# Down units of one plain chunk moved to its front, and attention pieces of the first two GLU chunks ordered behind the gate's multiplication

## The chip, the cores and the metric

The kernel runs on one core of a Trainium2 chip. The metric is the device time of the whole program in microseconds (us). The engines are called as in the profile: PE (TensorE matmuls) and PEld (its weight loads), DVE (VectorE), ACT (ScalarE), POOL (GpSimd) and SP (SyncE, which here only issues DMAs). L766 is line 766 of the kernel before; line numbers after the change are a few higher.

## The reference

The input is one sequence of 2048 tokens of width 576, in float32:

```python
h  = x + attn(layernorm(x)) @ wo          # 32 heads of 18, window of 8 keys at distances 0, 2, ..., 14
g  = layernorm(h) @ w_gate                # 576 x 4608
u  = layernorm(h) @ w_up                  # 576 x 4608
h2 = h + (sigmoid(g) * u) @ w_down        # 4608 x 576
```

## The kernel before

The tokens are split by even and odd position and by half into four blocks of 512. Every product is made from split operands: `split` rounds the source on ACT to a high part (L104) and subtracts on DVE for the low part (L105), and a product is three matmuls: high by high, low by high, high by low. So each weight, each activation and each hidden tile costs one ACT and one DVE instruction ahead of its matmuls.

The kernel has three stages. An opening normalises the input and makes q, k and v, with the first attentions beneath it. Then comes the GLU, whose 4608 columns are 36 chunks of 128, in an order written out in `items`. Chunks 0 to 11 are plain chunks ("std") that work for one block only; chunks 12 to 35 are "pair" chunks, which treat two blocks by a scheme of seven products instead of eight, on sums and differences of the blocks' activations (`X["s2"]`, `X["s3"]`, `X["s1"]` and so on); the same order is then run for the other two blocks.

A plain chunk is `single` (L777 on): a gate product of 14 matmuls into PSUM tile b1, its sigmoid on ACT (L790), an up product of 14 matmuls into b2, and `hidden` (L765), which multiplies the two on DVE (L766) and splits the result into h0h and h0l. b1 and b2 have one buffer each: the next chunk's up product may not begin before L766 has read b2.

Every second chunk, the down projection of two chunks is put into `queue` as a generator of four units. One unit (`down_tile`, L860) is 12 matmuls and one add into `stage` (L870). `single` calls `late`, by the name `units`, twice in a chunk: `late(1)` takes one unit, or two where a finished generator still stands ahead of another. Thus even chunks from 4 on take three units and odd ones the remaining unit in the first call, and the second call in an odd chunk only finds the generator finished.

Between its products a chunk calls `side(0)` to `side(5)`, here `twice`, which advances a background generator `bg` by one or two steps through `bg_step`. In the first 12 chunks that is `under_first`: what is left of the attention of block 1, piece by piece, then from chunk 5 on its output projection (`proj_scr`), and then `operands`, the sums that the pair chunks read. One attention has 16 yields: for each half of its tokens a product q times k (L189, 2304 elements a partition), an empty step and a reduction (L193); the softmax (L201 to L207) in two steps; for each half the product with v (L215), an empty step, and two folds (L221, L223). The last add (L226) and the write of the result on POOL's queue (L228) come with the step that begins the next attention and issues its q, k and v loads on SP (L176 to L178). When chunk 0 begins, one piece (L223) and the last add of one attention are left, and two whole attentions after it. Chunk 0 takes eight such steps: L223; then L226 with L189 of the first half, and an empty one; L193; L189 of the second half; after L766 in the program an empty one and L193; and the softmax's first step.

The order on each engine is not the order of the program. A planner lists the instructions ahead of time by priority and by when it expects them to be ready; `high_priority(HC)` or `(HI)` lifts what stands under it, and the engine then runs its list strictly in that order. `issue_after(ins)` orders all instructions written under it behind `ins` on the engine of `ins`, here DVE, without adding a wait on another engine. `skip` names the sides at which `bg_step` does nothing while attention is under way.

Buffers: the raw weights of a chunk come through `load_gu` (L702, tile wg, two buffers, two chunks ahead); the split weights w1 have two buffers, w2 and w4 one each; the split down weights d have four, so those of chunks 10 and 11 take the places of chunks 6 and 7, whose units chunk 8 and chunk 9 finish.

Of the kernel before, what the change touches and what calls it, by code (L numbers as in the profile page):

```python
# [18 lines left out]
ALU = mybir.AluOpType  # L19
# [31 lines left out]
END = object()  # L51
# [3 lines left out]
NSTD = 12  # L55
# [5 lines left out]
def kernel(ctx, tc, x, wqkv, wo, wmlp, out):  # L61
    nc = tc.nc
    dve, act, pool, pe, sp = nc.vector, nc.scalar, nc.gpsimd, nc.tensor, nc.sync

    def sb_pool(name, side="left"):
        return tc.tile_pool(name=name, bufs=1, side=side, reuse_waits="tile")
# [233 lines left out]
    def x_half(raw, rest):  # L300
        t = tl_tile() if rest is None else th_tile()
        split(t[:, 0:2], t[:, 2:4], raw)
        if rest is not None:
            split_rest(t[:, 4], rest)
        return t
# [394 lines left out]
    def load_gu(f, eng=sp, n=WC):  # L700
        ws = gw.tile([P, WC], F32, bufs=2, name="wg")
        behind[0] = eng.dma_start(ws[:, :n], wmlp[f][:, :n])  # L702
        return ws

    def paced(dst, src):
        with tc.issue_after(getattr(behind[0], "ins", behind[0])):
            behind[0] = sp.dma_start(dst, src)
# [33 lines left out]
    def prod(ps, xx, w, n, first):  # L741
        wt, k0 = w[n]
        k = 0
        for c in range(2):
            for a, m in ((0, 0), (0, 2), (1, 0)):
                pe.matmul(ps, wt[:, a, k0 + c], xx[:, m + c], start=first and k == 0,  # L746
                          stop=k == 5, skip_group_check=True)
                k += 1

    def rest(ps, xx, w, n):  # L750
        wt, k0 = w[n]
        for a in range(2):
            pe.matmul(ps, wt[:, a, k0], xx[:, 4], start=False, stop=a == 1,  # L753
                      skip_group_check=True)
# [3 lines left out]
    def halves(name, src):  # L758
        n = 3 if name == "h0" else gc_bufs
        hh = gc.tile([P, TB], F32R, bufs=n, name=name + "h")  # L760
        hl = gc.tile([P, TB], F32R, bufs=n, name=name + "l")
        split(hh, hl, src)
        return hh, hl

    def hidden(sg, ps, name):  # L765
        dve.tensor_tensor(sg, sg, ps, ALU.mult)  # L766
        return halves(name, sg)

    def s_tile():
        return gh.tile([P, TB], F32, tag="s", bufs=4, name="s")  # L770

    def b_tile(i):
        return gp.tile([P, TB], F32, name=f"b{i % 3 + 1}")
# [7 lines left out]
    def single(X, w, t, units, side):  # L781
        xa, xb = (X["a00"], X["a01"]) if t == 0 else (X["a10"], X["a11"])
        pg, pu = b_tile(0), b_tile(1)
        prod(pg, xa, w, "b00", True)
        side(0)
        prod(pg, xb, w, "b10", False)
        rest(pg, xb, w, "g4")
        sg = s_tile()
        with tc.high_priority(HC):
            act.activation(sg, pg, AF.Sigmoid)  # L790
        side(1)
        units(1)
        side(2)
        prod(pu, xa, w, "b01", True)
        side(3)
        prod(pu, xb, w, "b11", False)
        rest(pu, xb, w, "u4")
        with tc.high_priority(HC):
            hid = hidden(sg, pu, f"h{t}")
        side(4)  # L800
        units(1)
        side(5)
        return {t: hid}

    added = [None]
    gated = [None]
# [218 lines left out]
    def under_first():  # L1025
        wos = [None, None]
        for _ in ag:
            if c >= 3 and wos[1] is None:
                wos[1] = wos_early()
            yield ATT  # L1030
        at_stk.close()
        a1 = xt.tile([P, 5, TB], F32, tag="th", bufs=3, name="ar")
        with sb_pool("pj", "right") as pj:
            while c < 5:
                yield
            yield from proj_scr(pj, 1, a1, wos)
        with sb_pool("pp", "right") as pp:
            yield from operands(pp, 0, X, ("s2", "s3", "s1", "a11", "s4"), None, a1)
# [3 lines left out]
    c = 0  # L1042
# [35 lines left out]
    def bg_step(i):  # L1078
        nonlocal raw, phase
        if phase is ATT and i in skip:  # L1080
            return
        r = next(bg, END)
        phase = ATT if r is ATT else None
        if isinstance(r, dict):
            raw = r

    def finish_bg():
        while True:
            r = next(bg, END)
            if r is END:  # L1090
                return
            if isinstance(r, dict):
                set_raw(r)
# [7 lines left out]
    def units(n):  # L1101
        for _ in range(n):
            while queue:
                if next(queue[0], END) is END:
                    queue.pop(0)
                else:
                    break
# [6 lines left out]
    bg = under_first()  # L1114
# [70 lines left out]
    def last_sums(f):  # L1185
        def last(h0, h1):
            if f % 2 == 0:
                M["a00"] = halves("h0", hid_raw("00", *h0))
                hid_raw("10", *h1)
            else:  # L1190
                M["a01"] = halves("h0", hid_raw("01", *h0))
                hid_raw("11", *h1)
        return last
# [17 lines left out]
    def lag(n):  # L1211
        for _ in range(n):
            yield
# [22 lines left out]
    def twice(i):  # L1236
        bg_step(i)
        if i in (1, 4) or phase is not ATT and i in (2, 5):
            bg_step(i)

    for c, (kind, p, f) in enumerate(items):
        w, d = wc
        for b, late_c in ((0, NF + NSTD - 3), (1, NF + NSTD + 5)):
            if c == late_c:
                e, hf = BLOCKS[b]
                paced(ov[e, hf], hacc[b])
        skip = () if kind == "std" else (3,)
        by_seven = c >= NF + NSTD
        if c == NSTD:
            finish_bg()  # L1250
            last_x = splits[-1]
            bg = under_rest(getattr(last_x, "ins", last_x))
        if c == NF + NSTD:
            finish_bg()
            with tc.high_priority(HI):
                for n in ("s1", "a11"):
                    Xn[n] = x_half(*raw[n])
            X = Xn
            pp_stk.close()
            dw = ctx.enter_context(sb_pool("dw", "right"))  # L1260
        if c == 0:
            wc = wc_next
        elif c + 1 < len(items):
            wc = weights(items[c + 1][0], wg, c + 1 < NF + NSTD)
        if c + 2 < len(items):
            wg = load_gu(items[c + 2][2], n=WC if c + 2 < NF + NSTD else GU)
        hid = {}
        blocks = [p] if kind == "std" else [2 * p, 2 * p + 1]

        def last(h0, h1):  # L1270
            hid[0] = hidden(*h0, "h0")
            hid[1] = hidden(*h1, "h1")

        if kind == "std":
            hid = single(X, w, p, late, twice)
        elif not by_seven:
            side = last_pair if c == NF - 1 else bg_step

            def between(i):
                if i in (4, 6):  # L1280
                    units(2)
                side(i)

            pair(X, w, between, last)
        else:
            def between(i):
                nonlocal st, gc, gc_bufs, dk
                units(1)
                if c == NF + NSTD and i == 5:
                    assert not queue  # L1290
                    st_stk.close()
                    gc_stk.close()
                    gc = gc_stk.enter_context(sb_pool("gc2"))
                    st = st_stk.enter_context(sb_pool("st2"))
                    dk = dk_stk.enter_context(sb_pool("dk", "right"))
                    for n in ("s4h", "s4l", "s1h"):
                        dk.tile([P, TB], F32R, name=n)
                    gc_bufs = 2
                down_side(f, i)

            pair(X, w, between, last if f >= NF - NPL else last_sums(f))
            if f < NF - NPL:
                if f % 2:
                    if f == 1:
                        queue.append(lag(LAG))
                    queue.append(seven())
                continue
            d = M[f]
        seg.append((hid, d))
        if len(seg) == 2:  # L1310
            if by_seven and f == NF - NPL + 1:
                queue.append(load_tails())
            for b in blocks:
                queue.append(down_std(seg, b, f // 2) if kind == "std" else
                             down_tail(seg, b, f == NF - 1) if by_seven else down_units(seg, b))
            seg = []
# [44 lines left out]
```

## Time and profile before

| | us |
|---|---|
| three runs | 1581.74, 1587.62, 1590.11 (median 1587.62) |
| the profiled execution | 1584.15 |
| its span, from first to last instruction | 1582.2 |
| PE busy | 1551.0 (98%) |
| DVE busy | 1256.3 (79%) |
| ACT busy | 881.1 (56%) |
| mean granted clock of PE | 0.996 |

The plain chunks for the first block run from about 221 to 358 us. In a timeline row the first number is the start, the second the duration (from the first start to the last end, where several instructions are merged), then come engine, line, operation and tiles; in square brackets stands how long the engine was idle before it, and what ended that. A row by stages gives the window, its length, then the busy time of PE, PEld, DVE, ACT and POOL with instruction counts, the granted clock, the share of DMA time and GB/s.

### The profile page before, as it was taken

What the parts mean: (1) busy time and instruction counts of PE and PEld (TensorE: products, weight loads), DVE (VectorE), ACT (ScalarE), POOL (GpSimd) and SP (SyncE); (2) the same over time, 40 slices, a digit from 0 to 9 for tenths busy, and PEclk for the clock granted to TensorE, in tenths of its full rate; (3) what the DMA queues carried; (4) which work ended last, traced back from release to release, by engine and by line L of the source; (5) the groups of instructions that cost most, each with busy time, mean ns of one, the idle gap of its engine ahead of it and who ended that gap; (6) DMA issues with size and microseconds to landing.
All of it is one profiled execution on the core that took longest, in us unless ns stands there. A gap on an engine that the chain in (4) does not pass through costs nothing.

```text
span 1582.2 us, 22358 instructions
## 1 busy us (share of the span) xinstructions
PE 1551.0 (98%) x8520; PEld 1378.4 (87%) x8520; DVE 1256.3 (79%) x1883; ACT 881.1 (56%) x1584; POOL 199.0 (13%) x249
## 2 busy tenths in 40 slices
PE   8999989999999999999999999999999999999998
PEld 7899878887888888888888888888888888888888
DVE  6998999869999999999526588876777776677755
ACT  6631234425655655555543445767777776677761
POOL 2300000020000010000101010112112211112210
PEclk9999999999999999999999999999999999999999
DMA  8646544645457667664584524899999989989983
GB/s 276 216 168 220 186 185 166 222 165 171 118 147 195 166 170 186 165 165 109 138 239 151 181 81 126 185 180 177 171 180 186 175 169 185 176 169 181 185 175 121
DMA packets 77148, 273.96 MB, mean 173 GB/s; under 512 B 8336, under 2 KB 14224, under 8 KB 76144
## 3 DMA queue, kind: packets, MB, share of 16 engines
q0 software_dynamic: 28192, 107.29, 37.6%
q1 hardware_dynamic: 41216, 145.11, 27.2%
q10 hardware_dynamic: 7632, 20.12, 3.3%
q8 instruction: 66, 1.08, 0.3%
q14 instruction: 42, 0.34, 0.1%
HBM read 143.98 MB, written 130.87 MB: 174 GB/s over the span
## 4 chain that ended last, share of the span: by engine, by line
PE 85%; DVE 9%; DMA 4%; ACT 1%; issue 1%; POOL 0%; ACTq 0%; SPq 0%; POOLq 0%; DVEq 0%
PE b L746 43%; PE dp L860 15%; PE dp L922 11%; PE b L753 8%; PE acc L157 4%; DMA wg<-in_wmlp_dram 2%; DVE lg L193 2%; DVE pr L189 2%; PE b L157 1%; PE bgp L157 1%; DVE pr L215 1%; DMA kw<-k 1%; DMA h<-z 1%; DVE pr L221 1%; DMA k<-ev 1%
## 5 line engine op out<-in xcount | busy, mean ns | idle before, releaser
L746 PE MATMUL b<-tl,w 128*128 128x512 f32 x1704 | 433.5, 394 | 3.6 <-ACT s L816 2.0
L746 PEld LDWEIGHTS b<-tl,w 128*128 128x128 f32 x1704 | 309.4, 189 | 60.8 <-ACT s L816 3.1
L746 PE MATMUL b<-th,w 128*128 128x512 f32 x1344 | 346.9, 393 | 3.1 <-DVE s L766 3.1
L746 PEld LDWEIGHTS b<-th,w 128*128 128x128 f32 x1344 | 245.3, 188 | 48.3 <-DVE s L766 3.6
L928 ACT ACTIVATE ev<-dp 128x576 f32<-128x576 f32 x224 | 144.7, 646 | 63.0 <-PE dp L922 58.6
L753 PE MATMUL b<-th,w 128*128 128x512 f32 x568 | 176.3, 391 | 0.0
L104 ACT ACTIVATE w<-wg 128x384 fp32r<-128x384 f32 (+1 forms) x186 | 110.7, 601 | 112.7 <-PE b L753 54.4
L931 POOL DMA_DIRECT2D h<-ev x128 | 110.1, 860 | 458.5 <-ACT ev L928 444.7
L157 PE MATMUL acc<-qw,th 128*128 128x432 f32 x512 | 154.4, 362 | 3.0 <-DVE th L109 2.2
L105 DVE TENSOR_TENSOR w<-wg,w 128x384 fp32r<-128x384 f32 (+1 forms) x186 | 121.0, 656 | 38.4 <-ACT w L104 38.0
L105 DVE TENSOR_TENSOR w<-tw,w 128x512 fp32r<-128x512 f32 x120 | 82.6, 688 | 82.1 <-ACT w L104 81.4
L753 PEld LDWEIGHTS b<-th,w 128*128 128x128 f32 x568 | 107.0, 188 | 23.3
L860 PE MATMUL dp<-d,h1h 128*128 128x288 f32 x640 | 118.8, 295 | 0.0
L860 PE MATMUL dp<-d,h0h 128*128 128x288 f32 x608 | 112.1, 295 | 0.7 <-DVE tail L870 0.7
L868 ACT ACTIVATE stage<-dp 128x576 f32<-128x576 f32 x104 | 67.2, 647 | 71.4 <-PE dp L860 70.7
L157 PEld LDWEIGHTS acc<-qw,th 128*128 128x128 f32 x512 | 96.9, 189 | 8.7 <-DVE th L109 3.4
L860 PEld LDWEIGHTS dp<-d,h1h 128*128 128x128 f32 x640 | 98.7, 188 | 3.0
L104 ACT ACTIVATE w<-tw 128x512 fp32r<-128x512 f32 x120 | 75.4, 628 | 42.6 <-PE b L746 39.9
L860 PEld LDWEIGHTS dp<-d,h0h 128*128 128x128 f32 x608 | 93.9, 189 | 4.0 <-DVE tail L870 1.0
L157 PE MATMUL acc<-qw,tl 128*128 128x432 f32 x256 | 92.8, 363 | 0.1
L189 DVE TENSOR_TENSOR pr<-kw,q 128x2304 f32<-128x2304 f32 x32 | 81.8, 2555 | 9.7 <-DMA kw<-k 9.5
L876 POOL DMA_DIRECT2D h<-stage x26 | 31.0, 1193 | 438.5 <-ACT stage L868 337.3
(310 smaller groups left out, 2953.4 us busy)
## 6 DMA issues: line engine op xcount, KB each, us to landing
h<-ev POOLq DMA_DIRECT2D x96, 576.0 KB, 6.9
wg<-in_wmlp_dram SPq DMA_DIRECT2D x47, 928.0 KB, 5.8
h<-stage POOLq DMA_DIRECT2D x26, 1152.0 KB, 10.7
wg<-in_wmlp_dram SPq DMA_DIRECT2D x36, 640.0 KB, 4.2
kw<-k SPq DMA_DIRECT2D x16, 792.0 KB, 4.8
vw<-v SPq DMA_DIRECT2D x16, 792.0 KB, 4.7
wd<-in_wmlp_dram SPq DMA_DIRECT2D x18, 576.0 KB, 7.4
h<-ev POOLq DMA_DIRECT2D x32, 288.0 KB, 6.8
```

Source lines behind the costliest of these rows:

```text
L104: act.activation(hi, src, AF.Copy)
L105: splits.append(dve.tensor_tensor(lo, src, f32(hi), ALU.subtract))
L157: pe.matmul(ps[:, :n], a[:, c, js], m[:, c], start=k == 0, stop=False)
L189: dve.tensor_tensor(pr, both(kw, u), q[:, us].unsqueeze(2).broadcast_to([P, 2, W, CG]), ALU.mult)
L193: dve.tensor_reduce(lg[:, us].rearrange("p j w h -> p (j w h)"), pr.rearrange("p j w (h d) -> p (j w h) d", d=DH), AX.X, ALU.add)
L746: pe.matmul(ps, wt[:, a, k0 + c], xx[:, m + c], start=first and k == 0, stop=k == 5, skip_group_check=True)
L753: pe.matmul(ps, wt[:, a, k0], xx[:, 4], start=False, stop=a == 1, skip_group_check=True)
L860: pe.matmul(ps[:, i, :DH2], a[:, js], d[:, m, i * DH2:(i + 1) * DH2], start=k == 0, stop=k == n)
L868: act.activation(hv, ps, AF.Copy)
L922: pe.matmul(ps[:, i, :DH2], a[x][:, js], m[y], start=k in (0, 1, 3) and q == 0, stop=q == 2, skip_group_check=True)
L928: act.activation(hs[:, k % 2], ps[:, :, :DH2], AF.Copy)
L931: pool.dma_start(hsev[:, u, k0:k + 1], hs[:, :k + 1 - k0], accum_op=ALU.add, max_dma_last_dim=8 * D)
```

## The change

Two edits. In chunk 9 (`c == NSTD - 3`, the third-last plain chunk of the first pass) the call for down units that stood after `side(1)` stays, the one after `side(4)` is dropped, and one is added between the two halves of the gate product. So the one unit that is left there is issued at the front. In chunks 0 and 1 every attention step that is taken once a gate multiplication exists is written under `issue_after` of the latest one; `hidden` now records that multiplication in `gated`. In chunk 0, attention also takes no step at sides 2 and 3.

```diff
     def hidden(sg, ps, name):
-        dve.tensor_tensor(sg, sg, ps, ALU.mult)
+        m = dve.tensor_tensor(sg, sg, ps, ALU.mult)
+        gated[0] = getattr(m, "ins", m)
         return halves(name, sg)
...
         prod(pg, xa, w, "b00", True)
         side(0)
+        if c == NSTD - 3:
+            units(1)
         prod(pg, xb, w, "b10", False)
...
         side(4)
-        units(1)
+        if c != NSTD - 3:
+            units(1)
         side(5)
...
-        r = next(bg, END)
+        with ExitStack() as way:
+            if c < 2 and gated[0] is not None:
+                way.enter_context(tc.issue_after(gated[0]))
+            r = next(bg, END)
         phase = ATT if r is ATT else None
...
-        skip = () if kind == "std" else (3,)
+        skip = ((2, 3) if c == 0 else ()) if kind == "std" else (3,)
```

## The prediction

> **What bounds the kernel.** I read the page first, then who waits for whom on the matmul engine, then the timeline where those waits lie.
>
> ```profile
> span 1582.2 us, 22358 instructions
> PE 1551.0 (98%) x8520; PEld 1378.4 (87%) x8520; DVE 1256.3 (79%) x1883; ACT 881.1 (56%) x1584; POOL 199.0 (13%) x249
> ```
> PE is busy 1551.0 of 1582.2 us, and the change neither adds nor removes a matmul. So it can only win back PE's idle time and what follows from it, or add to it.
>
> ```profile
> PE b L746 <- DVE s L766: 8.4, 3, 4.0
> ```
> The largest wait of a GLU product is for L766, the gate's multiplication: three waits, 8.4 us. Now the first of the three, in chunks 0 and 1:
>
> ```profile
> 225.44 2.55 DVE L193 TENSOR_REDUCE lg<-pr 128x128 f32<-128x2304 f32 x1
> ...
> 227.02 0.62 PE L753 MATMUL b<-th,wf 128*128 128x512 f32 x2
> ...
> 228.38 2.55 DVE L189 TENSOR_TENSOR pr<-kw,q 128x2304 f32<-128x2304 f32 x1
> ...
> 230.19 0.61 PE L753 MATMUL b<-th,wf 128*128 128x512 f32 x2
> ...
> 231.52 2.55 DVE L193 TENSOR_REDUCE lg<-pr 128x128 f32<-128x2304 f32 x1
> 234.09 0.69 DVE L766 TENSOR_TENSOR s<-s,b 128x512 f32<-128x512 f32 x1
> ...
> 234.84 2.93 PE L746 MATMUL b<-tl,wf 128*128 128x512 f32 x6 [4.03 <-DVE s L766]
> ```
> Chunk 0's up product ends at 227.64 (227.02 + 0.62), so its multiplication could start there. DVE takes its instructions in the order written, and three attention pieces stand ahead of it, so it starts at 234.09. Chunk 1's gate product ends at 230.80; its up product needs the bank that the multiplication reads, and waits 4.03 us.
>
> ```profile
> 234.84 5.49 PE b L746 x12
> ...
> 250.38 2.75 PE b L746 x12
> ```
> From the chain that ended last: the twelve products after that wait take 5.49 us, twelve like them at 250.38 take 2.75. The wait thus costs 2.74 us more in slow matmuls, 6.77 in all.
>
> The other two waits lie where the plain chunks give way to the pair chunks:
>
> ```profile
> 330.22 0.52 PE L860 MATMUL dp<-d,h0h 128*128 128x288 f32 x2
> ...
> 331.30 1.47 ACT L104 ACTIVATE d<-wg 128x576 fp32r<-128x576 f32 x2 [0.20 <-PE dp L860]
> ...
> 335.30 0.63 PE L753 MATMUL b<-th,w 128*128 128x512 f32 x2
> ...
> 337.23 0.56 DVE L105 TENSOR_TENSOR w<-wg,w 128x384 fp32r<-128x384 f32 x1
> ...
> 337.81 0.33 SPq L702 DMA_DIRECT2D wg<-in_wmlp_dram  x1
> ...
> 344.99 0.61 PE L753 MATMUL b<-th,w 128*128 128x512 f32 x2
> ...
> 348.54 0.69 DVE L727 TENSOR_TENSOR tw<-wg 128x512 f32<-128x512 f32 x1 [6.77 <-DMA wg<-in_wmlp_dram]
> ...
> 352.36 0.68 DVE L766 TENSOR_TENSOR s<-s,b 128x512 f32<-128x512 f32 x1
> ...
> 353.18 1.61 PE L746 MATMUL b<-tl,w 128*128 128x512 f32 x6 [1.21 <-DVE s L766]
> ...
> 359.71 1.22 DVE L105 TENSOR_TENSOR tl<-ar,tl 128x1024 fp32r<-128x1024 f32 x1
> ...
> 361.98 0.68 DVE L766 TENSOR_TENSOR s<-s,b 128x512 f32<-128x512 f32 x1
> ...
> 362.72 2.60 PE L746 MATMUL b<-th,w 128*128 128x512 f32 x6 [3.14 <-DVE s L766]
> ...
> 365.97 4.55 PE L746 MATMUL b<-tl,w 128*128 128x512 f32 x18
> ```
> Chunk 9's remaining down unit starts at 330.22, behind the projection. The splits of two down weights wait for it on ACT (331.30). The up product of chunk 9 ends at 335.93; only then can chunk 10's single-buffered w4 be split (337.23 to 337.79), and that split is the last reader of the buffer into which the load at 337.81 goes. DVE stands still 6.77 us for this load, with chunk 10's multiplication behind it: due at 345.60 (344.99 + 0.61), it starts at 352.36. PE then waits 1.21 and 3.14 us.
>
> ```profile
> 362.00:380.00 18.00, 17.28 (x86) 15.04 (x87) 16.17 (x27) 8.96 (x15) 0.00 (x0) 0.91 0.53 205
> ```
> The granted clock over these 18 us is 0.91: another 18 x 0.09 = 1.62 us. The boundary costs 1.21 + 3.14 + 1.62 = 5.97 us. Both places together hold 12.7 us, the most that the change can bring by these rows.
>
> The Trainium skill, "TensorE: Matmul & The Clock Gate", Part 1, says that an idle window of about 3.4 us halves the clock and that some 3.4 us of work restores it. The trace agrees in kind: 4.03 us of waiting cost 2.74 more, 3.14 cost 1.62, and 1.21 left 1.61 us for six products. By that rule a new single wait above 3.4 us would cost an estimated 1.7 us on top, and the sum below would end 1.7 us higher.
>
> **The ties in chunks 0 and 1.** Nothing is removed; DVE's order changes. Counted along the generator's yields, chunk 0 now gets L193 of the first half, L189 of the second and (the third row above, at 231.52) L193 of the second half, two of them ahead of its multiplication in the program. Afterwards steps 2 and 3 are skipped, so only L189 of the first half stays ahead; it was done before 225.44. The rest carries the tie. The multiplication starts near 227.7, chunk 1's up product at 230.80, and 6.77 us return. A wait is added: behind the multiplication stand the tied pieces, DVE has only two short weight splits left from 225.4 to 227.7 and idles for about 1 us of it, and everything of attention waits for that. The next multiplication is at worst one 2.55 us piece late and is needed only after chunk 2's gate product, so I price that at nothing; without that cover it would be 2.55.
>
> The price is the attention's end.
>
> ```profile
> 234.84:298.46 63.62, 63.62 (x328) 55.53 (x329) 61.71 (x77) 32.22 (x53) 0.71 (x1) 0.96 0.42 148
> ```
> ```profile
> L105 DVE TENSOR_TENSOR w<-wg,w 128x640 fp32r<-128x640 f32 (+2 forms) x21 | 12.1, 598 | 0.6 <-ACT w L104 0.5
> ...
> L870 DVE TENSOR_TENSOR stage<-stage,dp 128x576 f32<-128x576 f32 x8 | 6.0, 748 | 0.0
> ...
> L105 DVE TENSOR_TENSOR h0l<-s,h0h 128x512 fp32r<-128x512 f32 x7 | 4.8, 686 | 0.0
> L766 DVE TENSOR_TENSOR s<-s,b 128x512 f32<-128x512 f32 x7 | 4.8, 683 | 0.3 <-PE b L753 0.2
> L105 DVE TENSOR_TENSOR d<-wg,d 128x576 fp32r<-128x576 f32 x6 | 4.5, 751 | 0.0
> ```
> ```profile
> 297.71 0.75 DVE L226 TENSOR_TENSOR kw<-kw 128x576 f32<-128x576 f32 x1
> ...
> 302.37 1.75 SPq L707 DMA_DIRECT2D oj<-o  x4
> ```
> DVE is busy 61.71 of the 63.62 us to the attention's end (297.71 + 0.75 = 298.46). The chunks' own work there is 12.1 + 6.0 + 4.8 + 4.8 + 4.5 = 32.2, about half. With PE 6.77 us ahead, 0.5 x 6.77 = 3.4 us of it comes earlier, and attention, which gets the other half, ends 3.4 / 0.5 = 6.8 us later by the clock. The idle microsecond ahead of the tie adds to it: (3.4 + 1.0) / 0.5 = 8.8. Bounds: 3, if DVE's present gaps (1.9 us) and short pieces take up most; (3.4 + 5.1) / 0.5 = 17, if two tied pieces of 2.55 us leave DVE idle for their full length. I take 8.8, since DVE has next to no gap. The projection's loads follow that end (302.37).
>
> SP is in order too:
>
> ```profile
> 251.24 0.32 SPq L178 DMA_DIRECT2D vw<-v  x1
> 252.30 0.33 SPq L702 DMA_DIRECT2D wg<-in_wmlp_dram  x1
> ```
> The v window waits for an attention piece on DVE, and chunk 5's weights are queued behind it. A few us later here is hidden by PE's two chunks of distance, between 0 and 2 us; I take 0.
>
> **The unit of chunk 9.** The projection's products lie ahead of it on PE, and the loads of that time meet the zero writes:
>
> ```profile
> 315.25 1.59 PE b L157 x12
> ...
> 328.18 1.58 PE bgp L157 x12
> ...
> 340.16 9.63 DMA h<-z
> ...
> 370.98 3.18 PE dp L860 x24
> ```
> Of the two calls that move, one finds only the finished generator; one unit of 12 matmuls goes from 330.22 to between the two halves of chunk 9's gate product. PE's total stays. Its add on DVE and the down weights' splits (1.47 on ACT and their halves on DVE) leave the crowded stretch from 330 to 337; the unit's tile of PSUM is free by then, as its last but one is added. No DMA is issued by it. Alone, with PE's order as it is, chunk 9's up product would still end at 335.93 and the load would come at most 1.5 us sooner: the low bound, about 1. With the projection 8.8 us later, however, PE finds the up product of chunk 9 before the projection's products (315.25 to 329.8), w4 is free up to 15 us earlier, and the load lands before the crowd: the whole 5.97. I take this one, because the late attention forces that order.
>
> **What is late next.** The pair chunk's second sum. Its split ends at 360.93 (359.71 + 1.22), its product is the second third of the row at 365.97, about 367.4. Without the 6.77 us of standing still it is ready at 354.2, plus 8.8 = 363.0; PE, 12.7 us earlier, wants it at 354.7. That is 8.3 us. PE can fill 3.2 of it with the two down units that now follow at 370.98 and depend on no sum; 5.1 remain. They fall in pieces on the first two sums, each near the waits of 1.21 and 3.14, so the clock adds between 0 and 1.6; I take 0.
>
> **Sum.** 6.77 + 5.97 - 5.1 = 7.6 us won. The profiled execution took 1584.15, with its span of 1582.2 and 1.95 around it: 1576.5. The median of the runs, 1587.62, lies 3.5 above it, inside their spread of 8.4; I stay with the profiled one and let the upper end hold the rest.
>
> **Rivals.**
> *All of it is kept.* DVE's gaps and an earlier start of the sums absorb the delay: 1584.15 - 12.7 = 1571.4. For it: around 345 DVE waits for a load rather than for work. Against it: it has nearly no gap before 298. 0.20.
> *It cancels.* The load stays behind the zero writes, so the second sum is ready at 360.9 + 8.8 = 369.7 against 367.4 - 6.8 = 360.6: 9.1 - 3.2 = 5.9 lost for 6.8 won, 1583.3. For it: a planner decides the order on PE and DVE, and here it put DVE behind a load. 0.15.
> *Slower.* The tied pieces leave DVE idle and attention ends 17 us late; the second sum comes at 377.9 against 360.6, 17.3 - 3.2 = 14.1 lost in one long wait, with 2.7 of slow matmuls behind it as at 234.84, for 6.8 won: 1594.2. It decides from an attention end about 15 us late (313.5 on). For it: DVE is full. Against it: weights and down adds can fill in. 0.13.
> That the tie does nothing can't be: L766 would have to stay behind pieces that are now ordered after it.
>
> **Chances.** The forecast has 0.52. About 0.5% (8 us) is what a measurement of this kernel can tell from no change. The forecast's own spread, 4 to 11 us won, lies half on either side of that: faster is 0.20 + 0.26 = 0.46, same 0.26 + 0.15 = 0.41, slower 0.13. The range goes from 1570 (all kept, less 1.4 of spread between runs) to 1590 (cancelled, at the level of the slower runs), and leaves out most of the slower case and a little below.
>
> **What would show it.** Right: the wait of 4.03 us and the slow products behind it gone; L766 of chunk 0 ahead of its L193; attention's last L226 some 3 to 10 us later by the clock; the load of chunk 12 issued well before the zero writes; a wait of PE at the pair chunk's first sums. Wrong: L226 near 298 with no wait after it (more won), a long wait of DVE for the weights still there (cancelled), or PE waiting for weights in chunks 2 to 6.

## The result, and the profile after

The changed kernel takes 1580.92 us (median of 22 runs, 1576.39 to 1588.99); the kernel before, in 22 runs beside them, 1584.88 (1581.46 to 1590.11). The ratio is 0.9978, 95% interval 0.9969 to 0.9987: about 3.5 us less (0.0022 x 1584.88), 2 to 5 by the interval. 7.6 us were forecast.

The profiled execution of the changed kernel took 1584.01 us, above that median, and has the same span as the one of before. Its page:

```profile
span 1582.2 us, 22347 instructions
PE 1551.0 (98%) x8520; PEld 1377.3 (87%) x8520; DVE 1255.2 (79%) x1883; ACT 879.2 (56%) x1584; POOL 199.9 (13%) x249
```

Equal spans hide what moved. The start of the k-th matmul, set against the k-th of before, shows it: from the 1000th to the 1300th (198.7 to 262.5 us of before) PE wins 6.2 us; from there to the 2000th (391.3) it gives 2.3 back on balance; to the 2150th (419.6) another 2.9; after that the two programs are the same, and differ only as executions do. First the front, in the timeline:

```profile
227.15 0.69 DVE L766 TENSOR_TENSOR s<-s,b 128x512 f32<-128x512 f32 x1 [1.25 <-PE b L753]
227.75 2.55 DVE L193 TENSOR_REDUCE lg<-pr 128x128 f32<-128x2304 f32 x1
...
229.60 0.62 PE L753 MATMUL b<-th,wf 128*128 128x512 f32 x2
...
230.05 1.52 PE L746 MATMUL b<-tl,wf 128*128 128x512 f32 x6
```

L766 of chunk 0 now stands ahead of its L193, and chunk 1's up product follows its gate product with no wait. DVE's idle time for the tie is the 1.25 us in brackets.

Next, who waits for whom on PE. The row for L766 (8.4 us in three waits) is gone altogether. Of the next two rows the first is new, and the second has grown (L820 is L816 of the kernel before, where the row had 2.0 us in two waits, the longest 1.8):

```profile
PE b L146 <- DMA oj<-o: 4.2, 1, 4.2
PE b L746 <- ACT s L820: 3.2, 3, 2.4
```

The first lies where the attention hands over to its projection:

```profile
307.78 0.75 DVE L226 TENSOR_TENSOR kw<-kw 128x576 f32<-128x576 f32 x1
...
309.27 0.33 SPq L702 DMA_DIRECT2D wg<-in_wmlp_dram  x1
309.46 0.82 POOL L230 DMA_DIRECT2D o<-kw  x1
...
311.01 0.61 PE L753 MATMUL b<-th,w 128*128 128x512 f32 x2
...
314.63 0.42 PE L864 MATMUL dp<-d,h0h 128*128 128x288 f32 x2
314.89 0.29 PE L864 MATMUL dp<-d,h0l 128*128 128x288 f32 x1
...
316.44 1.75 SPq L707 DMA_DIRECT2D oj<-o  x4
...
319.42 1.11 PE L146 MATMUL b<-ident,oj 128*128 128x128 f32 x4 [4.23 <-DMA oj<-o]
```

Attention ends at 308.53. POOL's queue then writes its last result, and the projection's first load (316.44) waits for that write to land, 6.85 us in the chain of waits. In the same moment, at 309.27, SP has sent the 928 KB of a chunk's weights (chunk 11's, counting on from chunk 5's load). Chunk 9's up product ends at 311.62 (the row at 311.01, found by counting products from chunk 0), so the projection does stand behind it in PE's list now. Its first transposes (L146) stand in chunk 10, three matmuls into a down unit. PE is there at 315.2, and 4.23 us pass with the rest of that unit and chunk work queued behind. The DMA issues of 292 to 326 us, first before, then after (KB and us to landing last):

```profile
o<-kw POOLq DMA_DIRECT2D x1, 128.0 KB, 2.9
```
```profile
o<-kw POOLq DMA_DIRECT2D x1, 128.0 KB, 6.9
```

By stages (window, length, busy time of PE, PEld, DVE, ACT, POOL, then the clock):

```profile
314.31:317.73 3.42, 0.88 (x6) 0.56 (x4) 1.49 (x2) 1.79 (x3) 0.00 (x0) 1.00 0.18 16
317.73:321.14 3.41, 1.72 (x8) 1.72 (x9) 0.00 (x0) 0.57 (x1) 0.00 (x0) 0.50 0.92 327
321.14:324.55 3.41, 3.41 (x16) 3.35 (x16) 1.50 (x3) 0.98 (x3) 0.00 (x0) 0.50 1.03 402
```

For 6.8 us after the wait's middle the clock is granted at half, and 1.72 + 3.41 us of PE's work in it take twice as long: 2.6 us more. The place costs 4.23 + 2.6 = 6.8 us.

The longest of the waits for L820, 2.37 us, lies behind a load of weights:

```profile
380.85 0.76 DVE L105 TENSOR_TENSOR d<-wg,d 128x576 fp32r<-128x576 f32 x1
...
381.67 0.33 SPq L702 DMA_DIRECT2D wg<-in_wmlp_dram  x1
...
390.53 0.74 ACT L104 ACTIVATE w<-wg 128x640 fp32r<-128x640 f32 x1 [4.38 <-DMA wg<-in_wmlp_dram]
...
392.68 0.57 ACT L820 ACTIVATE s<-b 128x512 f32<-128x512 f32 x1
...
393.31 3.01 PE L746 MATMUL b<-tl,w 128*128 128x512 f32 x12 [2.37 <-ACT s L820]
```

The load (chunk 15's by the same count; the expectations call it chunk 14's) lands after 8.8 us. ACT has the split of these weights ahead of L820 in its list, which copies a finished product out of PSUM, and stands 4.38 us; PE's next product goes into the bank that this copy reads, so PE needs the copy, not the weights, and stands 2.37. In the kernel before the load was sent at 379.75 and landed in 4.5 us. What differs is a transfer sent just ahead of it, in the DMA issues of after, 378 to 395:

```profile
h<-stage POOLq DMA_DIRECT2D x1, 1152.0 KB, 10.5
wg<-in_wmlp_dram SPq DMA_DIRECT2D x1, 928.0 KB, 8.8
```

### The profile page after: what moved, and what is told of

It is laid out like the page before. It is cut to its first block, busy times and chain, and to the rows that moved or that the text cites. A ratio compares the mean times of both kernels' runs of the same rounds, so it can differ in the third digit from the quotient of the medians.

```text
span 1582.2 us, 22347 instructions
## 1 busy us (share of the span) xinstructions
PE 1551.0 (98%) x8520; PEld 1377.3 (87%) x8520; DVE 1255.2 (79%) x1883; ACT 879.2 (56%) x1584; POOL 199.9 (13%) x249
## 4 chain that ended last, share of the span: by engine, by line
PE 58%; issue 16%; DVE 11%; DMA 8%; POOL 4%; ACT 2%; SPq 0%; ACTq 0%; POOLq 0%; DVEq 0%
PE b L746 27%; PE dp L864 13%; PE dp L926 6%; PE b L753 5%; PE acc L157 4%; POOL h L935 3%; DMA wg<-in_wmlp_dram 3%; DVE pr L189 2%; DVE pr L215 1%; DVE lg L193 1%; DVE w L105 1%; DVE pr L221 1%; PE b L157 1%; PE bgp L157 1%; DMA x<-tok 1%
## 5 line engine op out<-in xcount | busy, mean ns | idle before, releaser
L105 DVE TENSOR_TENSOR w<-wg,w 128x640 fp32r<-128x640 f32 (+1 forms) x186 | 120.8, 656 | 41.3 <-ACT w L104 41.1
```

What stands on the lines that cost most here:

```text
L105: splits.append(dve.tensor_tensor(lo, src, f32(hi), ALU.subtract))
```

## The experiments

The theory (A): the ties win the front, and by making attention late also the boundary, because PE's list then has chunk 9's up product ahead of the projection; the moved unit adds nothing; the price is the projection's first load, and what follows from it. The rivals differ in which part acts and where time is lost.

| kernel | ratio, 95% interval | PE against before, 1000th-1300th / -2000th / -2150th matmul, us |
|---|---|---|
| the change | 0.9978 (0.9969 to 0.9987) | -6.2 / +2.3 / +2.9 |
| ties and skip only | 0.9988 (0.9975 to 1.0001) | -6.1 / -1.7 / +4.4 |
| the same again | 0.9980 (0.9967 to 0.9992) | -5.8 / -0.6 / +4.4 |
| unit only | 1.0005 (0.9991 to 1.0019) | -0.1 / +2.4 / 0.0 |
| change, no skip | 1.0028 (1.0012 to 1.0044) | -3.6 / +5.8 / 0.0 |
| change, write by SP | 0.9990 (0.9977 to 1.0003) | -6.3 / -2.0 / +6.7 |
| change, projection from chunk 6 | 0.9954 (0.9938 to 0.9970) | -6.2 / -3.8 / +2.1 |
| the same again | 0.9952 (0.9935 to 0.9969) | -6.2 / -3.9 / +2.3 |
| ties, skip, projection from chunk 6 | 0.9974 (0.9959 to 0.9989) | -6.3 / -2.8 / +2.2 |
| the same again | 0.9962 (0.9946 to 0.9978) | -6.3 / -1.5 / +2.1 |
| before, projection from chunk 6 | 0.9993 (0.9980 to 1.0005) | -0.3 / -2.6 / +4.0 |
| change, sums on POOL | 0.9972 (0.9959 to 0.9985) | -6.4 / +4.2 / +0.6 |
| that, projection from chunk 6 | 0.9979 (0.9965 to 0.9993) | -6.3 / -0.6 / +6.0 |

The last column comes from one profile of each kernel, k-th matmul against k-th, good to about 1 us where the order differs; between profiles of unchanged code the 1000th matmul alone moves by up to 2.9 us, so only differences after it are used.

**The ties and the skip alone.**

```diff
-        if c == NSTD - 3:
-            units(1)
...
-        if c != NSTD - 3:
-            units(1)
+        units(1)
```

> Only the ties and the skipped steps of chunks 0 and 1; chunk 9's unit stays where it was. Theory A (late attention alone reorders PE, and the whole loss is one wait for the projection's first load): the 4.03 us wait at the front is gone as after the full change, attention ends about 10 us late, the first transpose still waits 4 to 5 us for its load, the two waits at the boundary for the gate's multiplication are gone although the unit was not moved; time within 1.5 us of the full change, 0.997 to 0.999 of before. Rival B (the moved unit is what clears the boundary): the waits of 1.2 and 3.1 us at the boundary are still there, some 5 us slower than the full change, 1.000 to 1.001 of before.

Measured: 0.9988; repeated, with this expectation:

> The change without the moved unit once more (12 runs gave 0.9988, 0.9975 to 1.0001, against 0.9978 with it). Theory A, the unit's place is worth nothing once the ties are there either: 0.997 to 0.999, and together with the first twelve runs within 0.001 of 0.9978. Rival C, the unit is worth 1.5 to 3 us beside the ties: 0.9985 to 1.000.

Measured: 0.9980. PE's waits of the first (the repeat has 2.5 and 2.8 in their places):

```profile
PE b L746 <- ACT s L817: 2.8, 2, 2.6
PE b L146 <- DMA oj<-o: 2.7, 1, 2.7
```

No wait for L766 is left, at the front or the boundary, though the unit stands where it stood. So both gains come from the ties and the skip. The wait at the projection is 2.7 us and not the 4 to 5 expected; the write of 128 KB ahead of it lands in 5.4 us here, against 6.9 in the change. Against the whole change the two results leave 1.6 and 0.3 us for the unit (0.0010 and 0.0002 of 1584), inside the intervals.

**The unit alone.** The diff of the change without its parts in `hidden`, `bg_step` and `skip`.

> Only the move of chunk 9's unit; attention as before. Theory A: the 4.03 us wait at the front is there, the projection's products still lie ahead of chunk 9's up product, chunk 12's load is issued at most 1.5 us sooner than 337.8, DVE still stands for it; 0 to 2 us won, 0.9985 to 1.000 of before. Rival B: the boundary's waits of 1.2 and 3.1 us vanish, about 6 us won, 0.996.

Measured: 1.0005, no difference, and the waits for L766 are the ones of before to the digit:

```profile
PE b L746 <- DVE s L766: 8.4, 3, 4.0
```

**The ties without the skip.**

```diff
-        skip = ((2, 3) if c == 0 else ()) if kind == "std" else (3,)
+        skip = () if kind == "std" else (3,)
```

> The change without its skipped steps: chunk 0 takes its attention steps at sides 2 and 3 again, the ties and the moved unit stay. Theory A: chunk 0's two pieces of 2.55 us that stand ahead of its multiplication in the program are not tied, so L766 of chunk 0 starts near 234 again and PE waits about 4 us there; what is gained is gained from chunk 1 on. Attention then ends nearer to 298 than to 308 (300 to 304), the projection's load is no longer late (no wait above 2 us for oj<-o), and the boundary decides: with PE's order as before the change 6 us are kept at most, ratio 0.997 to 1.001. Rival D, the ties alone clear the front and the skip is only there to spread the steps: the 4.03 wait is gone, ratio at 0.9978 or lower.

Measured: 1.0028, slower than before, outside both expectations. Attention ends at 299.67, hardly late, but:

```profile
231.89 1.66 PE L746 MATMUL b<-tl,wf 128*128 128x512 f32 x6 [1.49 <-DVE s L766]
...
308.25 1.11 PE L146 MATMUL b<-ident,oj 128*128 128x128 f32 x4 [3.04 <-DMA oj<-o]
...
354.82 1.60 PE L746 MATMUL b<-tl,w 128*128 128x512 f32 x6 [1.37 <-DVE s L766]
...
364.35 1.85 PE L746 MATMUL b<-th,w 128*128 128x512 f32 x6 [3.14 <-DVE s L766]
```

The front keeps 1.49 of its 4.03 us (about 4 expected), and both boundary waits are back (1.37 and 3.14; before 1.21 and 3.14), with chunk 9's up product behind the projection's products again (it ends at 337.3; 335.9 before, 311.6 in the change). The projection's load is waited for too, which was not expected: PE is 4 us early and the attention is not. This is the sharpest result: without lateness the boundary is not won, and being early at the projection costs what the front won. The skip is what makes the ties pay.

**The last write by SP's queue.**

```diff
-            pool.dma_start(oscr[b][:, :, g * CG:(g + 1) * CG], o)
+            eng = sp if (b, g) == (1, 3) else pool
+            eng.dma_start(oscr[b][:, :, g * CG:(g + 1) * CG], o)
...
-                pool.dma_start(oscr[b][:, :, D:DX], o[:, :, CG - DR:CG])
+                eng.dma_start(oscr[b][:, :, D:DX], o[:, :, CG - DR:CG])
```

> The full change, with the last attention's result written through SP's queue instead of POOL's. Theory A: the write lands some 3 us after its issue instead of 6.9, the projection's load follows 3 to 4 us sooner, the 4.2 us wait of the first transpose falls below 1.5 us and no slow matmuls follow it; 3 to 7 us won against the full change, 0.994 to 0.996 of before. Rival C (the pair chunk's sums are the price whatever the load does): the wait moves to the pair chunk's products, no change against the full change, 0.998.

Measured: 0.999, so the expected gain did not come, though the first part of its mechanism did:

```profile
o<-kw SPq DMA_DIRECT2D x1, 128.0 KB, 2.9
```
```profile
PE b L146 <- DMA oj<-o: 2.0, 1, 2.0
```

The write lands in 2.9 us as in the kernel before, and the wait falls from 4.23 to 2.0 (below 1.5 expected). The projection's load is now sent at 310.79, with a load of weights 2.3 us ahead of it, and takes 5.7 us to land in place of 2.9. PE reaches the 2000th matmul 4.3 us earlier than in the change, and gives 6.7 back by the 2150th: a wait of 2.79 us at 387.2 and halved clock from 390.0 to 396.9. The second place takes what the first releases.

**The projection one chunk later.**

```diff
-            while c < 5:
+            while c < 6:
                 yield
```

> The full change, with the projection's steps taken from chunk 6 on instead of chunk 5, so that PE's list has its first transposes 18 products and most of a unit (about 5 us) later, while the load itself comes when it did. Theory A: PE works through the 4.2 us in which it stood, no slow matmuls; 4 to 7 us won against the full change, 0.994 to 0.996 of before. Rival C: the projection's later steps come later too, and PE stands for the pair chunk's sums instead; 0 or a loss against the full change, 0.998 to 1.000.

Measured: 0.9954. PE's longest wait for oj<-o is 0.2 us, and the stage from 305 to 330 reads, first in the change, then here:

```profile
305.00:330.00 25.00, 20.77 (x104) 17.68 (x103) 14.49 (x26) 9.19 (x19) 1.45 (x2) 0.86 0.67 246
```
```profile
305.00:330.00 25.00, 24.84 (x141) 21.52 (x140) 21.30 (x37) 12.25 (x25) 1.45 (x2) 1.00 0.71 256
```

PE does 141 matmuls in place of 104. The attention ends at 312.84 by this profile's clock, which is 3.5 us behind that of the change at the 1000th matmul already, so it is about as late as there; but the transposes stand later in PE's list (321.21), and PE does not wait for them. With the sole hindrance at that place gone, the change is worth 7.3 us (0.0046 x 1584; 5 to 10 by the interval), close to the 7.6 forecast (whether by its working is asked below). It beats the kernel before; its interval and that of the change (0.9969 to 0.9987) barely touch. Its repeat:

> The kernel with the putting off to chunk 6 once more, in five rounds beside the two others, since its six runs and the twelve without the moved unit (0.9974, 0.9959 to 0.9989) overlap. Theory A, the unit's place is worth nothing: 0.9955 to 0.998, the same as without it. Rival C, the unit is worth 2 to 3 us here: 0.9945 to 0.996.

Measured: 0.9952.

**The same line on the kernel before.**

> The kernel before, with the projection's first step put off from chunk 5 to chunk 6 (the one line of the last experiment, without the change). Theory A: the kernel before has no wait for the projection's load (its write lands in 2.9 us, no row of oj<-o among PE's waits), its stall is the three waits for L766, 8.4 us, of which the front's 4.03 stays whatever happens at chunk 5. The later projection can at most free PE's order at the boundary, as the late attention did: between nothing and the 5.97 us of the boundary, so a ratio of 0.996 to 1.002, with the first of the three L766 waits kept in any case. If it gains nothing, the 1576.93 us of the last experiment needs the ties. Rival B: the putting off is the whole gain and the change adds nothing to it: 1576.9 here as well, ratio 0.9954.

Measured: 0.9993, no difference shown; rival B falls. PE's waits:

```profile
PE b L746 <- DVE s L766: 5.2, 3, 4.0
PE b L746 <- ACT s L816: 2.8, 3, 2.2
```

The front's 4.0 stays. Of the boundary's 4.35 us (1.21 + 3.14) at most 1.2 is left: a late projection clears it without any tie, which supports the reading that the order on PE, not the unit, is what matters there. The 2.6 us so won return at chunk 15's weights (the second row, with +4.0 in the table).

**The ties and the later projection, without the unit.** The diffs of the first and the fifth experiment together.

> The change without the moved unit, and the projection's first step put off to chunk 6. Theory A: the unit's place is worth nothing, so this is as fast as with it: a ratio of 0.994 to 0.997, no wait for oj<-o and none above 2 us for L766. Rival C: the unit, moved to the front, is what PE does instead of waiting once the projection is later; without it 1.5 to 4 us of waiting come back in chunks 9 to 12, ratio 0.997 to 1.000.

Measured: 0.9974, with a repeat:

> The ties and the putting off to chunk 6, without the moved unit, once more (0.9974, 0.9959 to 0.9989 in twelve runs, against 0.9954 and 0.9952 with the unit). Theory A: 0.994 to 0.9965, the difference was chance. Rival C: 0.9968 to 0.999 again, and the unit's place is worth some 3 us in this kernel.

Measured: 0.9962. Here the unit is not idle after all. Its first profile (the second has 2.6):

```profile
PE b L146 <- DMA oj<-o: 2.7, 1, 2.7
```

In both, PE again stands at the transposes; in both profiles with the unit at the front (0.9954, 0.9952) the wait is at most 0.2 us, since the transposes stand behind a whole unit. So with the later projection the unit covers a wait of 2.6 us. Rival C holds in the traces; the times agree (some 2.4 us between the means) but the intervals overlap, so its size stays open.

**Three of the pair chunks' sums on POOL.**

```diff
-        dve.tensor_tensor(s3, a00, a10, ALU.subtract)
+        eng.tensor_tensor(s3, a00, a10, ALU.subtract)
...
-        dve.tensor_tensor(s4, a01, s2, ALU.subtract)
+        eng.tensor_tensor(s4, a01, s2, ALU.subtract)
...
-        dve.tensor_tensor(rd, a0[:, 4], a1[:, 4], ALU.subtract)
+        eng.tensor_tensor(rd, a0[:, 4], a1[:, 4], ALU.subtract)
```

> The change with three of the five sums ahead of the pair chunks (L285, L287 and L289, 1.22, 1.22 and 0.69 us of DVE) done by POOL. Theory A: what the change gives back at chunk 14 (2.9 us between the 2000th and the 2150th matmul, of which 2.37 are a wait for a split of weights whose load SP issues at 381.67, released by DVE) comes from DVE, 17.70 of 18 us busy there. With 3.1 us taken from DVE that load is issued 2 to 3 us sooner and the wait falls below 1 us; the 4.23 us wait for oj<-o stays. Ratio 0.995 to 0.997. Rival E: POOL is slower and the sums get later, so PE waits in chunk 12 for a split of a sum, 2 us or more: ratio 0.998 to 1.001. Rival F: the load at chunk 14 is not DVE's doing; nothing moves, ratio 0.9978.

Measured: 0.9972, not to be told from the change. The test of DVE's part did not work, for two reasons in one profile:

```profile
354.94 2.81 POOL L285 TENSOR_TENSOR ar<-ar,ar 128x1024 f32<-128x1024 f32 x1 [1.16 <-DVE rs L283]
357.70 3.36 POOL L287 TENSOR_TENSOR rs<-ar,rs 128x1024 f32<-128x1024 f32 x1
```
```profile
382.08 0.33 SPq L702 DMA_DIRECT2D wg<-in_wmlp_dram  x1
```

A sum that takes DVE 1.22 us takes POOL 2.8 to 3.4, and PE now waits three times in chunk 12: 1.8 and 1.2 us for copies out of PSUM (L820, L830) and 1.2 for the split of a sum, so rival E holds in part (2 us or more for a sum's split). And the load that should have come 2 to 3 us sooner came at 382.08, against 381.67. With the later projection the same edit does not help either:

> The same three sums on POOL, with the projection's first step put off to chunk 6. Theory A: both places where the change gives time back are gone; against the putting off alone (0.9954) 1 to 2 us more, ratio 0.993 to 0.995. Rival E: sums on POOL too late, a wait in chunk 12, ratio 0.996 to 1.000.

Measured: 0.9979 (0.9965 to 0.9993), against 0.9952 (0.9935 to 0.9969) without it: likely worse, though the intervals just overlap. PE waits 1.2 and 1.4 us for splits of sums in chunk 12, and 2.9 us at 387.9 for the copy L820, which ACT has behind a load of weights; the stage around it has a clock of 0.83:

```profile
380.00:400.00 20.00, 17.11 (x68) 13.82 (x67) 14.50 (x19) 6.48 (x12) 0.00 (x0) 0.83 0.33 95
```

Whether a shorter DVE list at 350 to 380 would win chunk 15's wait is not shown; what both runs show is that PE waits for these sums when POOL makes them.

## Why the prediction was right or wrong

**The front: right.** 6.77 us were expected, 6.2 measured, and 5.8 to 6.4 in every kernel with ties and skip. L766 of chunk 0 starts at 227.15 (227.7 expected), chunk 1's up product at 230.05 (230.80, with the whole stretch 0.6 earlier in this profile).

**The boundary: right in its cause and its size.** DVE's standing still for the load, PE's waits of 1.21 and 3.14 and the half clock behind them are gone; chunk 12's load is sent at 320.85 instead of 337.81. That the late attention does this, and the unit alone does nothing, was the choice made there, and the first three experiments bear it out. This profile's account closes with the 6.0 us in full: 8.3 us were lost between the 1300th and the 2000th matmul (6.8 at the projection, and 0.86, 0.44 and 0.20 in three short waits), and 8.3 - 6.0 is the 2.3 of the table. The low bound of about 1 us for the unit alone was no measurable gain.

**The attention's end: right.** 8.8 us later by the clock was taken, 10.1 measured (308.53 against 298.46), within 3 to 17. The working holds in the main: from 222 us (221.35 in the change, whose profile is 0.65 early) to that end DVE is busy 82.49 us in place of 74.49, 8.0 more with the same attention in it, and idle 2.7 more; of the 8.8 worked out, 1.0 was idle time and the other 7.8 chunk work. What the skipped steps add to this was no term of its own, and they matter: without them the attention ends at 299.67, only 1.2 later.

**What is late next: this step failed, in two terms.** It looked for the first work that needs the late attention, named the pair chunk's second sum, and took 5.1 us off for it. It put the wait for the projection's load at nothing. It had noted that "the projection's loads follow that end", and rightly took the projection's products to stand behind chunk 9's in PE's list; but it did not set the moment at which PE comes to them there (315.2) against the moment at which their late load lands (319.4). That wait cost 4.23 + 2.6 us.

The second sum, on the other hand, cost next to nothing. PE came to it later than reckoned, after that wait, and between 340 and 385 us its only wait for a sum is this one:

```profile
PE b L746 <- ACT tl L104: 0.4, 1, 0.4
```
```profile
363.55 0.50 PE L746 MATMUL b<-tl,w 128*128 128x512 f32 x1 [0.44 <-ACT tl L104]
...
364.39 1.22 DVE L105 TENSOR_TENSOR tl<-ar,tl 128x1024 fp32r<-128x1024 f32 x1
```

Its split ends at 365.61, 2.6 us later than the 363.0 worked out, so the sum was late indeed. But even where PE has no wait at the projection in front of it, 5.1 us are not paid. With the projection one chunk later, this is the one wait for a sum in chunk 12:

```profile
368.55 2.57 PE L746 MATMUL b<-tl,w 128*128 128x512 f32 x10 [0.59 <-DVE tl L105]
```

There, 48 matmuls of down units stand in PE's list between 357.8 and 366.4, four units, where the prediction had counted on two to fill the time.

By the 2000th matmul 3.9 of the 7.6 us were won (6.2 - 2.3). Of these 2.9 went at chunk 15's weights, a place the prediction does not mention: a load 8.8 us under way beside a write of 1152 KB, and a split on ACT that stands ahead of a copy out of PSUM.

**The clock addition, taken as nothing, bounded by 1.6:** 2.6 us in this profile. The last section shows why no one value would have done.

**The test that tells**, the projection one chunk later, removes the wait at the projection and gives 7.3 us. So the size was lost there, and not at the front or in the boundary. That 7.3 lies so near the 7.6 forecast is in part luck: its profile keeps 7.9 us by the 2150th matmul (6.2 + 3.8 - 2.1), so 4.8 of the prediction's 12.7 are lost, about the 5.1 taken off, but only 0.6 of them in the wait for a sum and 2.1 at chunk 15's weights. How the change's own 3.5 us divide among the places is not settled: its profile shows one execution, in which 1.0 us was won by the 2150th matmul (6.2 - 2.3 - 2.9), and 22 of them lie between 1576.39 and 1588.99.

## What to carry to other kernels

When an edit makes a producer late, walk through its consumers in the order in which the engines' lists reach them, loads and stores between them included: the first one takes the price, and an engine that runs its list in order makes everything behind it pay. A gain in front of such a place is kept only if the place moves too; here one line that put the consumer back doubled the gain, and made no difference that could be measured without the change. And time a transfer beside what else is under way at its new moment, not by its landing in the profile of before.

## What the runs showed of the hardware

**Where a wait falls decides what it costs.** In the 14 traces the stretches at half clock (but for the last microseconds of each program) last 3.41 or 6.83 us, and within one execution their starts lie whole multiples of 3.413 us apart, as if one fixed row of windows ran through. With PE's idle time summed within such windows (after 200 us, the clock full): all 16 windows with 2.1 us or more of it were followed by a window at half clock, none of 23 with 1.2 to 1.79 was, and of 11 between 1.80 and 1.95 six were. Of 28 windows already at half clock, six were followed by another; these had 0.45 to 1.69 us idle, the other 22 at most 0.63. So one long wait across a border can cost no more than itself. A wait of 3.23 us, then its two windows:

```profile
1542.22 1.67 PE L746 MATMUL b<-th,w 128*128 128x512 f32 x6 [3.23 <-DVE s L839]
```
```profile
1537.40:1540.80 3.40, 1.58 (x7) 0.97 (x6) 0.59 (x1) 0.00 (x0) 0.00 (x0) 1.00 1.01 380
1540.80:1544.20 3.40, 1.98 (x9) 1.62 (x10) 2.49 (x3) 0.00 (x0) 0.00 (x0) 1.00 0.39 150
1544.20:1547.60 3.40, 3.34 (x25) 3.11 (x23) 3.40 (x6) 0.63 (x1) 0.00 (x0) 1.00 0.01 2
```

This is the repeat of the later projection: 1.8 and 1.4 us of idle time on either side of a border, and the clock stays at 1.00 throughout. In the kernel before, a wait of 1.8 us (448.8 to 450.6) lay within one window and the next ran at half clock. The two profiles of the ties and the skip alone show it in one kernel: a wait of 2.74 us at the projection, with 1.91 idle in its window, left the clock at 1.00; one of 2.80, with 2.51 in its window, was followed by 3.41 us at 0.50. A stretch of 6.83 us at half clock takes up to 3.4 us of PE's time (6.83 x 0.5), so by this estimate the same edit can cost up to 3.4 us more or less from one execution to the next, a part of the spread of every kernel here. The Trainium skill, "TensorE: Matmul & The Clock Gate", Part 1, says that the windows run freely and are 3413 ns long: the traces agree. It says that an idle window of about 3.4 us is what halves the clock; in these runs 1.80 to 1.95 us idle within a window was enough in six of 11 cases, and 2.1 in all.

**A transfer's landing depends on what is still under way when it is sent.** The write of 128 KB ahead of the projection landed in 2.9 us in the four traces in which no load of weights was under way when it was sent: the kernel before (the next load went 1.8 us after it), the unit alone, the later projection on the kernel before, and the write by SP, which sends in order with the loads. In the other ten, where such a load had been sent 0.2 to 3.5 us ahead and had not landed, it took 4.2 to 6.9. A load of 928 KB, chunk 15's, took 4.5 us in the three traces in which the write of 1152 KB was sent 2.8 us behind it. In eight in which that write had been sent 1.4 to 4.0 us ahead it took 8.0 to 11.7, but 5.3 in one in which it went 0.2 ahead. In the two of the change with the later projection it took 8.7 and 8.8 although that write had landed; writes of zeros and loads of attention's windows were under way there. Apart from the write by SP no experiment set these orders on purpose, so what slows the load is a reading of the traces.
